# GpSimd's folding of the late rows' output, taken out of one stretch and put in two pieces behind the last PC of two segments

## The chip, the cores and the metric

One core of a Trainium2 chip runs the whole program. The metric is the device time of one execution in microseconds. The kernel before has a median of 838.83 us over 3 runs (838.33 to 838.89). TensorE is called PE, VectorE DVE, ScalarE ACT, GpSimd POOL, and the queue that issues nearly all DMAs is SyncE's, SP.

## What is computed

One sequence of 2048 tokens with 512 features passes through two layers. The first is attention with a recurrent memory: the sequence is cut into 64 segments of 32 tokens, and each segment sees 8 memory rows and itself. The memory rows of its output are the memory of the next segment, so the segments form a chain. The second layer is an MLP with 1792 hidden features.

```
for s in range(n_seg):
    xs = x[:, s * seg_len:(s + 1) * seg_len, :]
    h = jnp.concatenate([mem, xs], axis=1)
    q, k, v = (einsum('btd,dhe->bhte', h, W) for W in (Wq, Wk, Wv))
    p = softmax(where(mask, einsum('bhqe,bhke->bhqk', q, k) * scale, -1e9))
    o = einsum('bhte,hed->btd', einsum('bhqk,bhke->bhqe', p, v), Wo)
    mem = o[:, :M, :]
    outs.append(o[:, M:, :])
h = x + concatenate(outs)                 # on layernorm(x)
out = h + gelu(layernorm(h) @ w1 + b1) @ w2 + b2
```

## The kernel before

**Tiling.** Four segments make a block of 128 tokens; 16 blocks, 64 segments, numbered from 0. Of each segment, 24 token rows and the 8 memory rows go through Q, K and V in the segment itself (`hT`). The last 8 token rows of the four segments of a block, the late rows, are projected together, a block ahead (`hB`), in fill-in work that stands between the chained matmuls: the first segment of a block (called the first, sg = 0) carries K of the late rows of the next block, the second carries Q, the third V, and the fourth the output projection of the block before, `wo_B`.

**One segment on the chained path.** PE does Q and K (line 864; they wait for the memory rows `hT`, line 1169), the scores SC0 and SC1 (line 1029, which wait for POOL's copy `ZC`, line 919), V, then the two halves of the probabilities times V (called PV0 and PV1, lines 1067 and 1072, which wait for DVE's `PTC`), PVA (line 1135, the rows of the segment before, which waits for POOL's copies `BD`, line 1124), and the output projection (line 1163). DVE makes the softmax of each half in two `PC` (line 1054) and one transposition `PTC` (line 1056), and at the segment's end transposes the output out of PSUM (`TT`, line 1175) and adds its halves into `hT` for the next segment and into `opT` for the output (line 1169). ACT empties PSUM (`kq`, `VS`, `OT`, line 882) and computes the exponentials.

**The tail of a segment** (`sa_tail`) is done while the next one runs: POOL scales the probabilities of the 24 rows (`PA`, line 1118, behind DVE's `rsa`), DVE transposes them (`PTA`, line 1120), and POOL copies them to `BD` in four copies.

**The folding.** `wo_B` leaves the late rows' output of a block in PSUM as four partial sums on four groups of 32 partitions. DVE transposes it to `TTB` (line 1194; one buffer for all blocks), and POOL folds it, in two halves of the feature columns. Each half is a copy of 64 partitions to `TTS`, an add of 64 partitions, a copy of 32 partitions, and four narrow adds of 32 partitions into `opT` (lines 1198 to 1204). `nat` then transposes `opT` with a DMA (`oN`, line 1209), adds it to x on DVE (line 1212), takes mean and variance and writes the sum to memory (line 1219).

**What sets the order.** Every operation is recorded with what it reads and writes. A list scheduler (`Sched.schedule`) orders each engine's work by planned times (`PLAN`), or by rank for what has none, and puts an operation into the earliest gap that it models. PE's order is written by hand (`ORDERS`). `align` counts PE's instructions and pads with weight loads, so that each segment starts at a given place (`PHASE`) within stretches of 256 instructions; `pauses` lets PE wait for one of its own earlier matmuls behind such a boundary, and `windows` places DMAs between boundaries. `EARLY` lists loads and transpositions for the MLP that are done in the last segments.

**The end.** The last `wo_B` within the loop (block 14's late rows) is in segment 63. Behind the loop, PE does the first MLP matmuls (line 1323) and, between them, `wo` of segments 62 and 63, PVA of segment 63 and `wo_B` of block 15. Then follow the second MLP matmuls (line 1520) and three more rounds of both (lines 1513 and 1520).

Of the kernel before, what the change touches and what calls it, by code (L numbers as in the profile page):

```python
# [21 lines left out]
SORT = True  # L22
FETCH_N, FETCH_US = 256, 0.0
FETCH_AT, PADS, SLIP = 65, 8, 24
PHASE = (4, 68, 132, 196)
KEEP = True
WINDOWS, WIN_LO, WIN_HI = True, 1.0, -0.8
PAUSES, PAUSE_IN, PAUSE_US = 3, 64, 0.5
# [3 lines left out]


EARLY = {54: (("hx", 0, 0.1), ("hx", 1, 0.6)), 55: (("hn", 0, 0.1), ("hn", 1, 0.4), ("hx", 2, 0.8)), 56: (("hx", 3, 0.3), ("hn", 2, 0.7)),
         57: (("hn", 3, 0.1), ("w1", 0, 0.6)), 58: (("w1", 6, 0.2),), 59: (("w1", 1, 0.1), ("w1", 2, 0.8)), 60: (("w1", 3, 0.2), ("w1", 4, 0.5)), 61: (("w1", 5, 0.1),)}
ORDERS = ((('Q0', 0, 1), ('K0', 0, 1), ('Q0', 1, 2), ('K0', 1, 2), ('Q0', 2, 3), ('Q1', 0, 1), ('Q0', 3, 4), ('K0', 2, 4), ('Q1', 1, 4), ('K1', 0, 4), ('SC0', 0, 99), ('V0', 0, 1), ('V1', 0, 1), ('V0', 1, 4), ('F1', 0, 1), ('SC1', 0, 99), ('V1', 1, 2), ('F0', 0, 1), ('V1', 2, 3), ('F1', 1, 2), ('V1', 3, 4), ('PV0', 0, 99), ('PVA', 0, 99), ('F1', 2, 3), ('WO', 0, 2), ('PV1', 0, 99), ('WO', 2, 8), ('F1', 3, 4), ('SA', 0, 99), ('F0', 1, 4)),
# [585 lines left out]
def build_kernel(nc, A_x, A_mem0, A_Wq, A_Wk, A_Wv, A_Wo, B_w1, B_b1, B_w2, B_b2, out):  # L622
# [3 lines left out]
    with st:  # L626
# [499 lines left out]
        def pv_a(s):  # L1126
            par = s % 3

            def f(e):
                for k in range(8):  # L1130
                    for t in range(2):
                        rows = slice(64 * t, 64 * t + 64)
                        c0 = 192 * (k // 4) + 24 * (k % 4)
                        o = quad[:, 2 + t, c0:c0 + 120].rearrange("p (b q) -> p b q", q=24)[:, 0:5:4]
                        ins = e.matmul(o, VS[rows, par, k // 4, (k % 4) * E:(k % 4 + 1) * E], BD[rows, s % 2, k // 2, 2 * t:2 * t + 2, :, k % 2],
                                       start=(k == 0), stop=True, tile_position=(64 * t, 0), skip_group_check=True)
                return ins
            S.op("pe", f, reads=[("VS", par, 0), ("VS", par, 1)] + [("BD", s % 2, j) for j in range(4)], writes=AQ, dur=0.29, mode=MH, ni=32)
# [47 lines left out]
        def wo_B(bk, bank):  # L1186
            for q in range(8):
                def f(e, q=q):
                    for j in range(4):
                        ins = e.matmul(ps[bank][32 * j:32 * j + 32, :], OTB[:, bk % 2, slot(8 * j + q), :], WO[:, 8 * j + q, :], start=(q == 0), stop=(q == 7),  # L1190
                                       tile_position=(0, 32 * j), skip_group_check=True)
                    return ins
                S.op("pe", f, reads=[("WO", g, a) for g in range(8) for a in range(2)] + [("OTB", bk % 2, sg) for sg in range(4)], writes=[("ps", bank)], dur=0.2135, mode=MC, ni=8)
            S.op("dve", lambda e: e.transpose(TTB[:].rearrange("p c q t -> p (c q t)"), ps[bank][:, :]), reads=[("ps", bank)], writes=["TTB"], dur=t_dve(512) + 0.02)
            o = opT[:, bk % 2, :, :].rearrange("p c (s t) -> p c s t", s=4)[:, :, :, NA:SEG]
            for c in (0, 2):
                t = TTB[:, c:c + 2]
                S.narrow(S.op("pool", lambda e, t=t: e.tensor_copy(TTS[0:64], t[64:128]), reads=["TTB"], writes=["TTS"], dur=0.7))
                S.narrow(S.op("pool", lambda e, t=t: e.tensor_tensor(t[0:64], t[0:64], TTS[0:64], ALU.add), reads=["TTB", "TTS"], writes=["TTB"], dur=0.7))
                S.narrow(S.op("pool", lambda e, t=t: e.tensor_copy(TTS[0:32], t[32:64]), reads=["TTB"], writes=["TTS"], dur=0.7))  # L1200
                for q in range(4):
                    def f(e, c=c, q=q, t=t):
                        x, y = [v[0:32, :, q].rearrange("p c (s t) -> p c s t", s=4) for v in (t, TTS)]
                        return e.tensor_tensor(o[32 * q:32 * q + 32, c:c + 2], x, y, ALU.add)
                    S.narrow(S.op("pool", f, reads=["TTB", "TTS"], writes=[("opB", bk % 2)], dur=0.3))

        def nat(bk):

# [139 lines left out]
        for s in range(NS):  # L1348
# [194 lines left out]
        rest = {0: lambda: wo(NS, later[-1], mem=False), 2: lambda: nat(NTB - 2), 4: lambda: pv_a(NS - 1), 5: lambda: pv_a_ev(NS - 1), 7: lambda: wo_B(NTB - 1, later[-1]),  # L1543
                9: lambda: wo(NS + 1, later[0], mem=False), 11: lambda: nat(NTB - 1)}
        rest = dict(zip((0, 1, 3, 4, 6, 7, 9), rest.values()))
        for n, fc in enumerate(range(3, FC)):
# [84 lines left out]
```

## Time and profile before

| | |
|---|---|
| median of 3 runs | 838.83 us (838.33 to 838.89) |
| the profiled execution's own time | 839.32 us |
| its span | 837.6 us |
| PE busy | 786.5 us, 94% of the span |
| DVE busy | 638.3 us, 76% |
| ACT busy | 534.6 us, 64% |
| POOL busy | 347.9 us, 42% |
| a segment in the middle of the program | 10.4 to 11.4 us |

The profile is of one execution; its times are counted from the start of its span. A row of the timeline gives start and duration in us, engine, line and operation, tiles and shapes, how many instructions were merged into it, and in brackets how long the engine stood idle ahead of it and what ended that. PE's matmuls overlap, so a row's duration reaches into the next row; distances are best read from start to start. A row of waits gives the waiting instruction, what it waited for, the sum in us, how often, and the longest.

### The profile page before, as it was taken

Reading aid. Unit: us, or ns where it says so; the run is one execution under the profiler, and the core shown is the slowest. Engines: PE = TensorE matmul, PEld = TensorE weight load, DVE = VectorE, ACT = ScalarE, POOL = GpSimd, SP = SyncE. Lnnn points to the kernel's source line nnn. Section 1 sums busy time; section 2 is a strip of 40 time slices with the busy share of each in tenths; the row PEclk is TensorE's granted clock in tenths of the full one; section 3 lists DMA queues with packets and bytes.
Section 4 is the critical chain, followed back from the end, with each engine's and each line's share of the span. In section 5 each row is a group of like instructions: output and inputs, shape, how many; then the busy total and the mean of one; then the engine's idle time right before and its main releaser. Section 6 shows DMA issues by size and latency. Waiting matters only on the chain.

```text
span 837.6 us, 43562 instructions
## 1 busy us (share of the span) xinstructions
PE 786.5 (94%) x19317; PEld 424.5 (51%) x18882; DVE 638.3 (76%) x2022; ACT 534.6 (64%) x1496; POOL 347.9 (42%) x886
## 2 busy tenths in 40 slices
PE   3788999999999999999999999999999999889998
PEld 1355555555555555555555555555555554534443
DVE  3367888989898989888989898989898887713111
ACT  2536767777776767676767676767676768723332
POOL 5023235453535353535353535353535343446200
PEclk9999999999999999999999999999999999989999
DMA  9950010101010101011010101010112130363200
GB/s 342 389 159 9 4 36 10 41 17 36 21 36 16 37 21 35 23 24 33 20 38 20 38 17 41 13 39 10 42 35 67 33 93 16 114 162 96 62 26 25
DMA packets 65450, 48.03 MB, mean 57 GB/s; under 512 B 29029, under 2 KB 61677, under 8 KB 65261
## 3 DMA queue, kind: packets, MB, share of 16 engines
q1 hardware_dynamic: 64928, 44.98, 18.3%
q8 instruction: 150, 2.46, 1.3%
q10 hardware_dynamic: 332, 0.27, 0.1%
q14 instruction: 40, 0.32, 0.1%
HBM read 31.08 MB, written 8.13 MB: 47 GB/s over the span
## 4 chain that ended last, share of the span: by engine, by line
PE 64%; DVE 18%; ACT 8%; SPq 5%; issue 2%; POOL 1%; DMA 1%; POOLq 0%; DVEq 0%
PE ps L864 28%; PE ps L1163 12%; PE quad L1520 6%; DVE PC L1054 5%; PE ps L604 5%; PE ps L1513 4%; ACT EC L1046 4%; PE quad L1067 3%; SPq L791 2%; ACT kq L882 2%; SPq L774 2%; DVE nmc L1037 2%; DVE KALL L905 2%; PE quad L1029 2%; PE ps L1097 1%
## 5 line engine op out<-in xcount | busy, mean ns | idle before, releaser
L864 PE MATMUL ps<-WQ,hT 128*32 128x512 bf16 x2048 | 157.0, 380 | 6.6 <-DVE hT L1169 5.4
L1163 PE MATMUL ps<-WO,OT 128*32 128x256 bf16 x4224 | 141.8, 275 | 1.8 <-issue 1.0
L864 PE MATMUL ps<-WV,hT 128*32 128x512 bf16 x1780 | 142.6, 379 | 0.0
L1118 POOL TENSOR_TENSOR PA<-SA,rsa 128x256 bf16<-128x256 f32 x64 | 39.8, 622 | 220.7 <-DVE rsa L1111 209.1
L883 ACT ACTIVATE kq<-ps 128x512 bf16<-128x512 f32 x146 | 87.2, 597 | 62.9 <-PE ps L864 62.6
L882 ACT CAST kq<-ps 128x512 bf16<-128x512 f32 x160 | 93.4, 583 | 37.3 <-PE ps L864 37.3
L1163 PEld LDWEIGHTS ps<-WO,OT 128*32 128x32 bf16 x4224 | 96.3, 96 | 24.8 <-ACT OT L882 2.6
L1054 DVE SCALAR_TENSOR_TENSOR PC<-EC,rsc,even 128x128 bf16<-128x128 f32 x256 | 98.9, 411 | 4.4
L1124 POOL COPY BD<-PTA 32x192 bf16<-32x192 bf16 x256 | 92.4, 361 | 16.3 <-DVE PTA L1120 0.5
L864 PE MATMUL ps<-WK,hT 128*32 128x512 bf16 x1292 | 92.7, 379 | 0.0
L864 PEld LDWEIGHTS ps<-WQ,hT 128*32 128x32 bf16 x2048 | 58.3, 96 | 63.0 <-issue 18.1
L1046 ACT ACTIVATE EC<-quad,nmc 128x64 f32<-128x64 f32 x252 | 77.1, 311 | 10.1 <-DVE nmc L1037 3.6
L905 DVE STREAM_TRANSPOSE KALL<-kq 128x256 f32<-128x256 f32 x160 | 69.6, 435 | 16.2 <-ACT kq L882 13.4
L882 ACT CAST OT<-quad 128x128 bf16<-128x128 f32 (+1 forms) x207 | 67.2, 353 | 20.4 <-PE quad L1072 11.7
L604 PE MATMUL ps<-WK,hT 128*32 128x512 bf16 x756 | 75.0, 379 | 0.4 <-ACT kq L883 0.4
L882 ACT CAST VS<-ps 128x512 bf16<-128x512 f32 x126 | 73.8, 586 | 1.8
L864 PEld LDWEIGHTS ps<-WV,hT 128*32 128x32 bf16 x1780 | 51.5, 96 | 34.5 <-issue 2.0
L1109 ACT ACTIVATE SA<-SA 128x256 f32<-128x256 f32 x64 | 26.7, 417 | 55.4 <-DVE SA L1108 53.1
L1516 ACT ACTIVATE WQ<-ps,b1t 128x512 bf16<-128x512 f32 x42 | 28.9, 687 | 51.9 <-PE ps L1513 51.9
L905 DVE STREAM_TRANSPOSE QT<-kq 128x256 f32<-128x256 f32 x128 | 56.3, 440 | 6.1 <-ACT kq L883 4.3
L864 PEld LDWEIGHTS ps<-WK,hT 128*32 128x32 bf16 x1292 | 37.0, 97 | 46.0 <-issue 20.5
L1175 DVE STREAM_TRANSPOSE TT<-ps 128x256 f32<-128x256 f32 x66 | 28.9, 438 | 35.5 <-PE ps L1163 35.3
(161 smaller groups left out, 1501.6 us busy)
## 6 DMA issues: line engine op xcount, KB each, us to landing
WV<-in_A_Wv_dram SPq DMA_DIRECT2D x4, 1024.0 KB, 10.3
WK<-in_A_Wk_dram SPq DMA_DIRECT2D x4, 1024.0 KB, 18.3
WQ<-in_A_Wq_dram SPq DMA_DIRECT2D x4, 1024.0 KB, 19.0
WO<-in_A_Wo_dram SPq DMA_DIRECT2D x16, 256.0 KB, 7.5
v_last<-VSB SPq DMA_DIRECT2D x60, 64.0 KB, 3.1
VBD<-v_last SPq DMA_DIRECT2D x60, 64.0 KB, 2.8
h_mid<-xr SPq DMA_DIRECT2D x16, 128.0 KB, 1.9
WQ<-h_mid SPq DMA_DIRECT2D x4, 512.0 KB, 4.2
```

The source lines that it names most:

```text
L604: return e.add_instruction(mybir.InstMatmult(name="I-%d" % (4000000 + _kept[0]), engine=mybir.EngineType.PE, start_tensor_calc=start, stop ...
L864: ins = e.matmul(o, l, m, start=(k == 0), stop=(k == DC - 1), tile_position=(0, 32 * j), skip_group_check=True)
L882: return {"act": (lambda e: e.copy(out, src), t_act(n, ps_)), "dve": (lambda e: e.tensor_copy(out, src), 0.155 + 1.0e-3 * n * fast)}
L883: return {"act": (lambda e: e.mul(out, src, scale_), t_act(n, ps_)), "dve": (lambda e: e.tensor_scalar(out, src, scale_, None, ALU.mult), ...
L905: S.op("dve", lambda e: e.transpose(out, src), reads=[("kq", i)], writes=[key], dur=t_dve(256) + 0.02)
L1046: return e.activation(EC[:, r, sl, :], o[:, sl, :], ACTF.Exp, bias=nmc[:, r, sl:sl + 1], accum_out=smc[:, r, sl:sl + 1])
L1054: S.op("dve", lambda e, sl=sl, xc=xc: e.scalar_tensor_tensor(PC[:, r, :, :, sl], xc, rsc[:, r, sl:sl + 1], ev, ALU.mult, ALU.mult), reads= ...
L1118: S.either({k: ((lambda e: e.tensor_tensor(PA[:].rearrange("p a t b -> p a b t"), SA[:].rearrange("p (a b) t -> p a b t", b=2), bc2, ALU.m ...
L1124: S.narrow(S.op("pool", lambda e, j=j, rows=rows: e.tensor_copy(BD[rows, par, :, j, :, :], PTA[rows, :, 0:NA, :]), reads=["PTA"], writes=[ ...
L1163: ins = e.matmul(ps[bank][32 * j:32 * j + 32, 0:256], lhs(slot(h)), wo_cols(h, b), start=(k == 0), stop=(k == 15), tile_position=(0, 32 * ...
L1513: ins = e.matmul(ps[bank][:, 0:SBT], W1[:, cc, fc * P:(fc + 1) * P], hnT_of(k)[:, cc, :], start=(cc == 0), stop=(cc == DC - 1))
L1520: S.op("pe", lambda e: e.matmul(quad[:, t, :], gT_of(k, fc)[:, t * P:(t + 1) * P], W2[:, fc, :], start=(fc == 0), stop=(fc == FC - 1)), re ...
```

## The change

The folding becomes two functions, one for each half of the feature columns (`chunk(0, ...)` and `chunk(2, ...)`), which `wo_B` only puts on a list. They are recorded in the tails of the next two segments, the first and the second of the following block, and each may start only when the last `PCa` and `PC` of that segment are done. In the last segment, 63, both are recorded and also wait for the four copies `BD` of that segment. The folding of block 15 is recorded right behind its `wo_B`, as before. `nat` of a block moves from the first to the third segment, behind the folding. `PHASE` is 4 instructions less everywhere, and one transposition and one load of `EARLY` come later.

```diff
-PHASE = (4, 68, 132, 196)
+PHASE = (0, 64, 128, 192)
...
-         57: (("hn", 3, 0.1), ("w1", 0, 0.6)), 58: (("w1", 6, 0.2),), 59: ...
+         57: (("w1", 0, 0.6),), 58: (("hn", 3, 0.2), ("w1", 6, 0.4)), 59: ...
...
-            for c in (0, 2):
+
+            def chunk(c, after):
                 t = TTB[:, c:c + 2]
-                S.narrow(S.op("pool", lambda e, t=t: e.tensor_copy(TTS[0:64], t[64:128]), reads=["TTB"], writes=["TTS"], dur=0.7))
+                S.narrow(S.op("pool", lambda e: e.tensor_copy(TTS[0:64], t[64:128]), reads=["TTB"], writes=["TTS"], dur=0.4, after=after))
...
+            folds.extend([lambda after: chunk(0, after), lambda after: chunk(2, after)])
+
+        folds = []
+
+        def fold(after=()):
+            tag, S.tag = S.tag, None
+            folds.pop(0)(after)
+            S.tag = tag
...
-            if sg == 0 and bk > 1:
+            if sg == 2 and bk > 1:
                 nat(bk - 2)
...
                 sa_tail(s)
+                if folds and s % 4 < 2 or s == NS - 1:
+                    for _ in folds[:1 if s < NS - 1 else 2]:
+                        fold([S.last_writer[(n, 1)] for n in ("PC", "PCa")] + [S.last_writer[("BD", s % 2, j)] for j in range(4 * (s == NS - 1))])
...
-        rest = {..., 7: lambda: wo_B(NTB - 1, later[-1]),
+        rest = {..., 7: lambda: (wo_B(NTB - 1, later[-1]), fold(), fold()),
```

How the instructions stand on POOL around the folding of one block, in the kernel before. The first row is the end of the first half, which follows the copies `BD` of the fourth segment; each `PA` opens the tail of one more segment, here that of the first, done while the second runs:

```order
L1204 TENSOR_TENSOR opT<-TTB,TTS 32x8x8 x4
L1198 COPY TTS<-TTB 64x256
L1199 TENSOR_TENSOR TTB<-TTB,TTS 64x256
L1200 COPY TTS<-TTB 32x256
L1204 TENSOR_TENSOR opT<-TTB,TTS 32x8x8
L1118 TENSOR_TENSOR PA<-SA,rsa 128x4x2x32
L1204 TENSOR_TENSOR opT<-TTB,TTS 32x8x8
L919 COPY ZC<-QT 128x8x2x8
L926 COPY ZC<-QTB 128x16x2x8
L919 COPY ZC<-QT 128x8x2x8
L1124 COPY BD<-PTA 32x4x48 x4
L1204 TENSOR_TENSOR opT<-TTB,TTS 32x8x8 x2
```

The same place with the change:

```order
L1124 COPY BD<-PTA 32x4x48 x4
L1199 COPY TTS<-TTB 64x256
L1200 TENSOR_TENSOR TTB<-TTB,TTS 64x256
L1201 COPY TTS<-TTB 32x256
L1205 TENSOR_TENSOR opT<-TTB,TTS 32x8x8 x4
L1118 TENSOR_TENSOR PA<-SA,rsa 128x4x2x32
L919 COPY ZC<-QT 128x8x2x8
L926 COPY ZC<-QTB 128x16x2x8
L919 COPY ZC<-QT 128x8x2x8
L1124 COPY BD<-PTA 32x4x48 x4
L1199 COPY TTS<-TTB 64x256
```

Before, both halves followed one another behind the copies `BD` of one segment's tail, and the last narrow adds stood between the next segment's `PA` and `ZC` and behind its `BD`. Now one half follows each of two segments' copies, none stands between `PA` and `ZC`, and its first copy waits for DVE as well.

POOL at the end of segment 63, before; the second row is the start of the folding of block 14:

```order
L1124 COPY BD<-PTA 32x4x48 x4
L1198 COPY TTS<-TTB 64x256
L1199 TENSOR_TENSOR TTB<-TTB,TTS 64x256
L1200 COPY TTS<-TTB 32x256
L1204 TENSOR_TENSOR opT<-TTB,TTS 32x8x8 x4
L1118 TENSOR_TENSOR PA<-SA,rsa 128x4x2x32
```

and with the change:

```order
L1124 COPY BD<-PTA 32x4x48 x4
L1118 TENSOR_TENSOR PA<-SA,rsa 128x4x2x32
L1124 COPY BD<-PTA 32x4x48 x4
L1199 COPY TTS<-TTB 64x256
L1200 TENSOR_TENSOR TTB<-TTB,TTS 64x256
L1201 COPY TTS<-TTB 32x256
L1205 TENSOR_TENSOR opT<-TTB,TTS 32x8x8 x4
```

`PA` and the copies `BD` of segment 63 have moved ahead of the two halves of the folding.

DVE at the same place, before and with the change (`WV` here is the normalised x of the MLP's second round, `TTB` in the last row that of block 15):

```order
L1111 RECIPROCAL rsa<-sma 128x8
L1169 TENSOR_TENSOR opT<-TT 64x4x24 x2
L1267 TENSOR_SCALAR WV<-WQ,agg,rst 128x512 x3
L1175 STREAM_TRANSPOSE TT<-ps 128x256
L1169 TENSOR_TENSOR opT<-TT 64x4x24 x2
L1267 TENSOR_SCALAR WV<-WQ,agg,rst 128x512
L1120 STREAM_TRANSPOSE PTA<-PA 128x128
```

```order
L1111 RECIPROCAL rsa<-sma 128x8
L1169 TENSOR_TENSOR opT<-TT 64x4x24 x2
L1276 TENSOR_SCALAR WV<-WQ,agg,rst 128x512
L1120 STREAM_TRANSPOSE PTA<-PA 128x128
L1276 TENSOR_SCALAR WV<-WQ,agg,rst 128x512
L1175 STREAM_TRANSPOSE TT<-ps 128x256
L1169 TENSOR_TENSOR opT<-TT 64x4x24 x2
L1276 TENSOR_SCALAR WV<-WQ,agg,rst 128x512 x2
L882 CAST OT<-quad 128x16x24
L1194 STREAM_TRANSPOSE TTB<-ps 128x512
```

`PTA` stands behind one normalisation instead of four and behind two adds instead of four. PE's matmuls stand in the same order in both kernels, but for four weight loads of padding less in segment 1.

More of the change, by code (lines that the diff above doesn't have):

```diff
@@ L1195, in wo_B, with f @@
             o = opT[:, bk % 2, :, :].rearrange("p c (s t) -> p c s t", s=4)[:, :, :, NA:SEG]
-            for c in (0, 2):
+            def chunk(c, after):
                 t = TTB[:, c:c + 2]
-                S.narrow(S.op("pool", lambda e, t=t: e.tensor_copy(TTS[0:64], t[64:128]), reads=["TTB"], writes=["TTS"], dur=0.7))
-                S.narrow(S.op("pool", lambda e, t=t: e.tensor_tensor(t[0:64], t[0:64], TTS[0:64], ALU.add), reads=["TTB", "TTS"], writes=["TTB"], dur=0.7))
-                S.narrow(S.op("pool", lambda e, t=t: e.tensor_copy(TTS[0:32], t[32:64]), reads=["TTB"], writes=["TTS"], dur=0.7))
+                S.narrow(S.op("pool", lambda e: e.tensor_copy(TTS[0:64], t[64:128]), reads=["TTB"], writes=["TTS"], dur=0.4, after=after))
+                S.narrow(S.op("pool", lambda e: e.tensor_tensor(t[0:64], t[0:64], TTS[0:64], ALU.add), reads=["TTB", "TTS"], writes=["TTB"], dur=0.73))
+                S.narrow(S.op("pool", lambda e: e.tensor_copy(TTS[0:32], t[32:64]), reads=["TTB"], writes=["TTS"], dur=0.41))
                 for q in range(4):
-                    def f(e, c=c, q=q, t=t):
+                    def f(e, q=q):
                         x, y = [v[0:32, :, q].rearrange("p c (s t) -> p c s t", s=4) for v in (t, TTS)]
                         return e.tensor_tensor(o[32 * q:32 * q + 32, c:c + 2], x, y, ALU.add)
-                    S.narrow(S.op("pool", f, reads=["TTB", "TTS"], writes=[("opB", bk % 2)], dur=0.3))
+                    S.narrow(S.op("pool", f, reads=["TTB", "TTS"], writes=[("opB", bk % 2)], dur=0.31))
+            folds.extend([lambda after: chunk(0, after), lambda after: chunk(2, after)])
[4 more added lines that the diff above has]
+            S.tag = tag
         def nat(bk):
@@ L1542, in build_kernel @@
         early, later = (free + sorted(set(busy)))[:2], (free + sorted(set(busy)))[2:]
-        rest = {0: lambda: wo(NS, later[-1], mem=False), 2: lambda: nat(NTB - 2), 4: lambda: pv_a(NS - 1), 5: lambda: pv_a_ev(NS - 1), 7: lambda: wo_B(NTB - 1, later[-1]),
+        rest = {0: lambda: wo(NS, later[-1], mem=False), 2: lambda: nat(NTB - 2), 4: lambda: pv_a(NS - 1), 5: lambda: pv_a_ev(NS - 1), 7: lambda: (wo_B(NTB - 1, later[-1]), fold(), fold()),
                 9: lambda: wo(NS + 1, later[0], mem=False), 11: lambda: nat(NTB - 1)}
```

2 lines of the change are left out of this document (1 added, 1 removed).

## The prediction

> **What bounds the kernel now.** I read the chain of waits first, then who waited for whom on PE, then the timeline of single segments against each other, then the end of the loop.
>
> ```profile
> PE 64%; DVE 18%; ACT 8%; SPq 5%; issue 2%; POOL 1%; DMA 1%; POOLq 0%; DVEq 0%
> PE quad L1067 <- DVE PTC L1056: 6.5, 25, 0.7
> PE quad L1135 <- POOL BD L1124: 4.7, 1, 4.7
> PE ps L1163 <- issue: 1.0, 2, 0.7
> PE ps L864 <- issue: 0.7, 3, 0.3
> ```
>
> PE carries most of the chain; the other engines count where they release it. One wait stands out: PE waited once for 4.7 us, at PVA, for POOL's copies `BD`. And 25 times it waited for `PTC` ahead of PV0 or PV1, 6.5 us in all.
>
> How long a segment is, from the first Q matmul of one to that of the next:
>
> ```profile
> 82.72 0.41 PE L864 MATMUL ps<-WQ,hT 128*32 128x512 bf16 x4 [0.77 <-DVE hT L1169]
> 93.55 0.40 PE L864 MATMUL ps<-WQ,hT 128*32 128x512 bf16 x4
> 103.86 0.41 PE L864 MATMUL ps<-WQ,hT 128*32 128x512 bf16 x4
> ...
> 403.38 0.41 PE L864 MATMUL ps<-WQ,hT 128*32 128x512 bf16 x4
> 413.75 0.41 PE L864 MATMUL ps<-WQ,hT 128*32 128x512 bf16 x4
> 424.11 0.41 PE L864 MATMUL ps<-WQ,hT 128*32 128x512 bf16 x4
> 435.48 0.40 PE L864 MATMUL ps<-WQ,hT 128*32 128x512 bf16 x4
> 446.00 0.41 PE L864 MATMUL ps<-WQ,hT 128*32 128x512 bf16 x4
> ```
>
> The row at 424.11 opens the first segment of a block: it lasts 11.37 us, the second (435.48) 10.52, the third (403.38) 10.37. The first three rows are the first and second segment of block 1, which have no folding yet: 10.83 and 10.31. So a first segment is 0.54 longer and a second 0.21 longer than without a folding and without the transposition into `TTB`, which stays. That is the ceiling of what the loop can give: 0.75 for each folding.
>
> ```profile
> L1204 POOL TENSOR_TENSOR opT<-TTB,TTS x128: 306/313/398, 132.5 to 750.8; 32x64 bf16<-32x64 f32 x128
> ```
>
> 128 narrow adds, 8 a folding, are 16 foldings: 14 lie in a first and second segment (blocks 2 to 15), one at the end of segment 63, one behind the loop.
>
> **The end of the loop.** In the last segment the folding is not beside the path but on it:
>
> ```profile
> 726.87 0.20 DVE L1111 RECIPROCAL rsa<-sma 128x8 f32<-128x8 f32 x1
> 727.10 0.96 DVE L1169 TENSOR_TENSOR opT<-TT 64x96 bf16<-64x96 f32 x2
> 728.07 1.25 DVE L1267 TENSOR_SCALAR WV<-WQ,agg,rst 128x512 bf16<-128x512 bf16 x3
> 734.04 0.31 DVE L1120 STREAM_TRANSPOSE PTA<-PA 128x128 f32<-128x128 f32 x1 [2.68 <-POOL PA L1118]
> ...
> 726.66 0.39 POOL L1198 COPY TTS<-TTB 64x256 f32<-64x256 f32 x1 [5.81 <-DVE TTB L1194]
> 733.38 0.62 POOL L1118 TENSOR_TENSOR PA<-SA,rsa 128x256 bf16<-128x256 f32 x1 [0.17 <-POOL opT L1204]
> 734.48 1.54 POOL L1124 COPY BD<-PTA 32x192 bf16<-32x192 bf16 x4 [0.48 <-DVE PTA L1120]
> ...
> 730.35 1.02 PE L1323 MATMUL ps<-xr,QTB 128*128 128x512 bf16 x4
> 736.08 0.50 PE L1135 MATMUL quad<-BD,VS 64*128 64x48 bf16 x16 [4.71 <-POOL BD L1124]
> 736.52 1.89 PE L1323 MATMUL ps<-xr,QTB 128*128 128x512 bf16 x4
> ...
> 82.00:92.00 10.00, 9.26 (x244) 5.56 (x299) 8.16 (x29) 6.61 (x20) 3.12 (x8) 1.00 0.01 3
> 736.00:741.70 5.70, 5.62 (x28) 2.02 (x28) 1.86 (x4) 1.85 (x3) 0.82 (x3) 0.50 0.77 130
> ```
>
> `rsa` is ready at 727.07, but POOL began the folding at 726.66 and takes `PA` only at 733.38. `PTA`, the copies `BD` and at 736.08 PVA follow, while PE had run dry 4.71 us earlier, at 731.37. The last two rows are from a table by stretches (the column behind POOL's is the granted clock): from 736.00 to 741.70 PE has a clock of 0.50, against 1.00 in an early stretch, and the same four matmuls take 1.89 us instead of 1.02. So the wait costs 4.71 and half of 5.7 behind it, 2.8: 7.5 us.
>
> With the change `PA` and `BD` come ahead of the folding. `PA` runs from 727.1 to 727.75. On DVE, `PTA` then stands behind two adds (0.96 at most, the row of before, which lay beside the folding) and one normalisation (1.25 for three, so 0.42): 727.07 + 1.38 + 0.31 = 728.8. The copies take 1.54: `BD` is ready at 730.3, and PE asks for it at 731.37. Cover 1.07 us; what exceeds it would be lost one for one. I take the whole **7.5 us**; the low end, if the wait only moves to another place, is in the rivals.
>
> What becomes late instead: the folding of block 14 (6.55 us, from 726.66 to `PA`'s 733.38 less 0.17) now runs from 730.3 to 736.9, 3.7 us later by the clock, with PE 7.5 earlier. On it hang `TTB` of block 15 (one buffer), and SP, which waits for it in order:
>
> ```profile
> 733.24 1.20 SPq L1209 DMA_TRANSPOSE oN<-opT  x1
> 734.49 5.19 SPq L1278 DMA_TRANSPOSE WQ<-WV  x4
> 745.66 3.38 SPq L1535 DMA_DIRECT2D WK<-in_B_w_dram  x4
> ...
> 761.26 4.66 PE L1513 MATMUL ps<-WQ,WK 128*128 128x512 bf16 x20
> ```
>
> The transposition of block 14's output moves from 733.24 to 737.0; behind it are the four transpositions for the MLP's second round (to 743.4) and, with a second such wait for the folding of block 15 (`TTB` from 737, then 6.55 of folding, to about 744.3), the last `w1` loads, issued by 749. PE wants the second round at 761.26 - 7.5 = 753.8: 4.8 us of cover for the first matmul, more for the late columns. Cost nothing; without that cover each us is lost.
>
> **The first segment.** The folding lies beside the softmax of the second half:
>
> ```profile
> 430.81 0.72 POOL L1199 TENSOR_TENSOR TTB<-TTB,TTS 64x256 f32<-64x256 f32 x1
> ...
> 409.90 0.63 DVE L1054 SCALAR_TENSOR_TENSOR PC<-EC,rsc,even 128x128 bf16<-128x128 f32 x2
> 430.97 1.18 DVE L1054 SCALAR_TENSOR_TENSOR PC<-EC,rsc,even 128x128 bf16<-128x128 f32 x2
> 434.84 0.49 DVE L1169 TENSOR_TENSOR hT<-TT 64x32 bf16<-64x32 f32 x2
> 444.17 0.53 DVE L1169 TENSOR_TENSOR opT<-TT 64x96 bf16<-64x96 f32 x2
> 445.06 0.45 DVE L1175 STREAM_TRANSPOSE TT<-ps 128x256 f32<-128x256 f32 x1 [0.37 <-PE ps L1163]
> 445.55 0.39 DVE L1169 TENSOR_TENSOR hT<-TT 64x32 bf16<-64x32 f32 x2
> ...
> 432.55 0.27 PE L1067 MATMUL quad<-PTC,VS 64*128 64x32 bf16 x8 [0.32 <-DVE PTC L1056]
> 431.93 1.26 ACT L882 CAST OT<-quad 128x384 bf16<-128x384 f32 x3
> 438.26 0.32 POOL L1204 TENSOR_TENSOR opT<-TTB,TTS 32x64 bf16<-32x64 f32 x1
> ```
>
> The two `PC` take 1.18 us beside POOL's adds and copies, 0.63 in the third segment. With the folding behind them 0.55 goes from DVE, of which PE can use the 0.32 that it stood idle ahead of PV1. Not all of that comes through: the third of ACT's three casts reads PV1's result, and ACT is busy with the other two, which don't, until about two thirds of 1.26, 432.8; the second half of the output projection waits for that cast. Of 0.32 I take **0.2** (bounds 0 and the 0.54 above). The memory adds at the end, 0.49 here against 0.39 at 445.55, keep their 0.10: half a folding is 3.3 us and now runs from about 431.6 to 434.9, so it still reaches them.
>
> **The second segment.** A narrow add of 0.32 no longer stands between `PA` and `ZC` (438.26), and none behind `BD`: at most the 0.21 above. But half a folding now runs from about 442.8 to 446.0, beside the adds at 444.17 and 445.55. Beside the folding two such adds took 0.96 (727.10), 0.43 more than here; the 0.37 that DVE idles ahead of `TT` hides that but for 0.06, and the memory adds get the 0.10 of the first segment. That leaves 0.21 - 0.16 = **0.05**; the low end, if the memory adds slow like those at 727.10 (0.39 x 0.96/0.53, 0.32 more), is -0.17.
>
> The rest of the edits I take as nothing. `nat`'s transposition moves to the third segment, its reader on DVE stands in the fourth, so a whole segment covers it. Of `EARLY`, one transposition moves by a segment, its reader is PE in segment 60; uncovered it would cost one such DMA issue (1.20) and its landing, once. `PHASE` moves the boundaries by four instructions: PE's waits on issue are 1.7 us in all, so at best that is gained, and I put the same on the other side.
>
> **Sum.** 14 x (0.2 + 0.05) = 3.5, and 7.5 at the end: 11.0 us. The profiled execution took 839.3 (837.6 of span and 1.7 around it), which gives 828.3; the median of the runs is 0.5 below the profiled one, so **827.8 us**.
>
> **The rivals.**
> 1. The loop gives nothing. POOL's half foldings slow the ends of two segments as much as they free the middle of one. For it: ACT's casts stand close behind DVE's chain, and the memory adds are the last link into the next segment. Against: block 1's segments are shorter. 838.8 - 7.5 = 831.3 us.
> 2. The loop gives its ceiling, 14 x 0.75 = 10.5: 838.8 - 7.5 - 10.5 = 820.8. Against: `TTB`'s transposition remains, and the half foldings still run.
> 3. The end only moves its wait: PE runs into the MLP's second round while SP still stands behind the two foldings. Price at most what SP's order allows: if the 749 above became 757, 3.2 us past 753.8: 831.0. For it: SP serves in order, and two of its entries now wait for POOL. For a wait that is shortened but not gone, the rows say that 0.77 of idling (at 82.72) leaves the clock at 1.00 (the stretch from 82 to 92) and 4.71 doesn't. The Trainium skill, "TensorE: Matmul & The Clock Gate", Part 1, puts the limit at about 3.4 us of idling; by it a wait of 3.2 would add no slow clock, and 831.0 would stand; the 4.71 agrees with it, and no row here shows a wait between.
> 4. Slower: in each of the 28 segments both memory adds are held until a narrow add of POOL (0.31) has ended, 0.62 instead of the 0.10 counted, about 0.5 more on the last link: 827.8 + 28 x 0.5 = 841.8. It decides from 0.4 a segment (11.0/28), and it stands in the row at 430.97, where a `PC` paid nearly double. Against: at 434.84 the adds met a copy and lost 0.10. The Trainium skill, "SBUF — State Buffer", section "SBUF: two separate sides", has this rule: a DVE operation with two SBUF inputs and a GpSimd operation that reads SBUF exclude each other for a whole instruction. By it this rival would be the forecast; the rows agree for `PC` and only in part for the memory adds.
>
> **Chances.** The forecast 0.63, with a range of its own of 824.5 to 830.5 (the boundaries' 1.7 and 1 to 1.5 of the loop on either side); rival 1 0.18, rival 2 0.07, rival 3 0.08, rival 4 0.04. The range of 8 in 10 is 823.5 to 831.8: above it takes in rivals 1 and 3, below a loop that gives 0.56 a folding (7.8) instead of 0.25 (3.5). What can be told from no change here is 0.2%, 1.7 us. Faster is everything but rival 4 and 0.02 of rival 3, for an end that gives all back: 0.94; the same 0.02; slower 0.04.
>
> **What would show it.** PVA of segment 63 without a wait and PE's clock at 1.00 through the end of the loop; `PA` there right behind `rsa`, about 6 us ahead of the folding's end. First segments of about 11.17 us, with the two `PC` at 0.63 and no wait ahead of PV1 larger than before; second segments of about 10.47, without POOL's add between `PA` and `ZC`, and with the two memory adds at about 0.5. The third and fourth as before. Wrong would be: memory adds of 0.6 or more, first segments of 11.3 or more, or a new wait of PE at line 1513.

## The result and the profile after

The changed kernel has a median of 829.28 us (828.36 to 829.8) beside 838.86 us of the kernel before; the ratio is 0.9886, interval 0.9869 to 0.9903. The same kernel in a later job: 828.32 us (827.85 to 829.45) beside 839.74, 0.9866 (0.9853 to 0.988). So it is some 10 us faster; forecast were 11.0 us and 827.8. The profiled execution took 829.1 us with a span of 827.4, 10.2 less than before.

**The waits of PE after the change** (engine, line, what it waited for, sum in us, times, longest):

```profile
PE ps L864 <- DVE hT L1169: 5.7, 8, 1.1
PE quad L1067 <- DVE PTC L1056: 2.3, 12, 0.2
PE quad L1029 <- POOL ZC L919: 2.1, 12, 0.2
```

Two rows are to be compared with before: the wait for `BD` (4.7) is gone from the list, and the 25 waits for `PTC` of 6.5 us have become 12 of 2.3.

**The end of the loop**, POOL, DVE and PE in the timeline (start, duration, engine, line):

```profile
724.02 0.20 DVE L1111 RECIPROCAL rsa<-sma 128x8 f32<-128x8 f32 x1
724.40 0.62 POOL L1118 TENSOR_TENSOR PA<-SA,rsa 128x256 bf16<-128x256 f32 x1 [6.40 <-DVE rsa L1111]
725.47 0.30 DVE L1120 STREAM_TRANSPOSE PTA<-PA 128x128 f32<-128x128 f32 x1
725.91 1.57 POOL L1124 COPY BD<-PTA 32x192 bf16<-32x192 bf16 x4 [0.89 <-DVE PTA L1120]
727.54 0.39 POOL L1199 COPY TTS<-TTB 64x256 f32<-64x256 f32 x1
...
732.53 1.49 POOL L1205 TENSOR_TENSOR opT<-TTB,TTS 32x64 bf16<-32x64 f32 x4
...
727.43 1.02 PE L1332 MATMUL ps<-xr,QTB 128*128 128x512 bf16 x4
728.38 0.37 PE L1135 MATMUL quad<-BD,VS 64*128 64x48 bf16 x16
728.69 1.04 PE L1332 MATMUL ps<-xr,QTB 128*128 128x512 bf16 x4
...
751.04 0.59 PE L1525 MATMUL ps<-WQ,WK 128*128 128x512 bf16 x2
```

And the same stretches as in before's table (length, busy time of PE, PEld, DVE, ACT and POOL with instructions, then the granted clock, DMA share, GB/s):

```profile
726.00:732.00 6.00, 6.00 (x51) 2.31 (x53) 2.58 (x7) 4.10 (x7) 5.15 (x13) 1.00 0.78 243
732.00:738.00 6.00, 6.00 (x104) 3.14 (x96) 2.32 (x5) 1.73 (x3) 4.28 (x12) 1.00 0.30 69
```

`PA` now stands right behind `rsa`, `BD` is ready at 727.48, and the folding runs from 727.54 to 734.02. PVA (728.38) has no wait in brackets, and PE is busy through both stretches at clock 1.00. From the first matmul with `QTB` to the first of the second round (line 1513, now 1525) it was 761.26 - 730.35 = 30.91 us and is 751.04 - 727.43 = 23.61: 7.30 us less, and no wait has come up at the second round.

**A first and a second segment** in the middle of the program, the openings on PE and then what DVE and POOL do within them:

```profile
422.52 0.41 PE L864 MATMUL ps<-WQ,hT 128*32 128x512 bf16 x4
433.74 0.40 PE L864 MATMUL ps<-WQ,hT 128*32 128x512 bf16 x4
444.16 0.41 PE L864 MATMUL ps<-WQ,hT 128*32 128x512 bf16 x4
454.53 0.41 PE L864 MATMUL ps<-WQ,hT 128*32 128x512 bf16 x4
...
429.38 0.63 DVE L1054 SCALAR_TENSOR_TENSOR PC<-EC,rsc,even 128x128 bf16<-128x128 f32 x2
433.04 0.55 DVE L1169 TENSOR_TENSOR hT<-TT 64x32 bf16<-64x32 f32 x2
443.68 0.41 DVE L1169 TENSOR_TENSOR hT<-TT 64x32 bf16<-64x32 f32 x2
...
430.13 0.39 POOL L1199 COPY TTS<-TTB 64x256 f32<-64x256 f32 x1 [1.46 <-DVE PC L1054]
430.61 0.72 POOL L1200 TENSOR_TENSOR TTB<-TTB,TTS 64x256 f32<-64x256 f32 x1
431.86 1.49 POOL L1205 TENSOR_TENSOR opT<-TTB,TTS 32x64 bf16<-32x64 f32 x4
```

The first segment lasts 11.22 (11.37 before), the second 10.42 (10.52), the third 10.37 as before. The two `PC` at 429.38 take 0.63 for 1.18 before, and POOL's folding begins just behind them. Its narrow adds (from 431.86 to 433.35) reach into the memory adds at 433.04, which take 0.55. All `PC` together, a row by line (busy time, mean ns of one):

```profile
L1054 DVE SCALAR_TENSOR_TENSOR PC<-EC,rsc,even 128x128 bf16<-128x128 f32 x256 | 90.5, 378 | 4.4
```

Summed over segments 8 to 59, the 13 first segments give 1.9 us, the 13 second ones 1.3 (0.55 of it from a single one that lasted 10.98 in before); the third ones cost 0.4. The fourth ones are 1.0 shorter, but this differs between executions: in part it hangs on whether the copies from `xT` on POOL meet a `PC`.

### The profile page after: what moved, and what is told of

It is laid out like the page before. It is cut to its first block, busy times and chain, and to the rows that moved or that the text cites. A ratio compares the mean times of both kernels' runs of the same rounds, so it can differ in the third digit from the quotient of the medians.

```text
span 827.4 us, 43568 instructions
## 1 busy us (share of the span) xinstructions
PE 786.6 (95%) x19317; PEld 425.3 (51%) x18878; DVE 637.3 (77%) x2022; ACT 530.9 (64%) x1496; POOL 349.0 (42%) x886
## 4 chain that ended last, share of the span: by engine, by line
PE 64%; DVE 19%; ACT 8%; SPq 5%; issue 2%; DMA 1%; POOL 1%; DVEq 0%; POOLq 0%
PE ps L864 27%; PE ps L1163 13%; PE quad L1532 6%; PE ps L604 4%; PE ps L1525 4%; ACT EC L1046 4%; DVE PC L1054 4%; ACT kq L882 3%; PE quad L1067 3%; SPq L791 2%; DVE KALL L905 2%; SPq L774 2%; DVE nmc L1037 2%; PE ps L1332 1%; PE ps L1097 1%
## 5 line engine op out<-in xcount | busy, mean ns | idle before, releaser
L864 PE MATMUL ps<-WQ,hT 128*32 128x512 bf16 x2048 | 160.1, 383 | 6.5 <-DVE hT L1169 5.7
L1124 POOL COPY BD<-PTA 32x192 bf16<-32x192 bf16 x256 | 94.4, 369 | 16.7 <-DVE PTA L1120 0.9
L864 PE MATMUL ps<-WK,hT 128*32 128x512 bf16 x1292 | 94.5, 381 | 0.0
L1054 DVE SCALAR_TENSOR_TENSOR PC<-EC,rsc,even 128x128 bf16<-128x128 f32 x256 | 90.5, 378 | 4.4
L1046 ACT ACTIVATE EC<-quad,nmc 128x64 f32<-128x64 f32 x252 | 76.8, 310 | 10.2 <-DVE nmc L1037 3.7
L604 PE MATMUL ps<-WK,hT 128*32 128x512 bf16 x756 | 76.7, 380 | 0.4 <-ACT kq L883 0.4
L1584 DVE TENSOR_TENSOR WV<-quad,WV 128x512 bf16<-128x512 f32 x16 | 11.1, 692 | 51.8 <-PE quad L1532 48.1
```

The costliest lines, as they stand in the source:

```text
L604: return e.add_instruction(mybir.InstMatmult(name="I-%d" % (4000000 + _kept[0]), engine=mybir.EngineType.PE, start_tensor_calc=start, stop ...
L864: ins = e.matmul(o, l, m, start=(k == 0), stop=(k == DC - 1), tile_position=(0, 32 * j), skip_group_check=True)
L1046: return e.activation(EC[:, r, sl, :], o[:, sl, :], ACTF.Exp, bias=nmc[:, r, sl:sl + 1], accum_out=smc[:, r, sl:sl + 1])
L1054: S.op("dve", lambda e, sl=sl, xc=xc: e.scalar_tensor_tensor(PC[:, r, :, :, sl], xc, rsc[:, r, sl:sl + 1], ev, ALU.mult, ALU.mult), reads= ...
L1124: S.narrow(S.op("pool", lambda e, j=j, rows=rows: e.tensor_copy(BD[rows, par, :, j, :, :], PTA[rows, :, 0:NA, :]), reads=["PTA"], writes=[ ...
```

## The experiments

Each has a ratio to the kernel before as it ran in the same job.

**1. The changed kernel again** (no edit).

> The changed kernel once more. Theory: the two stretches in which the profile of after granted half the clock in the opening (37.79 to 44.61 and 51.44 to 54.85 us) against one in before (42.01 to 45.42) come and go from run to run, and are no part of the change: the rounds scatter by about 1 us around 829.3 us, and a second profile shows another pattern, segments 0 and 1 shorter by up to 1.1 us. Rival: the change causes them (4 pad loads fewer in segment 1): the same stretches again, segments 0 and 1 again 1.1 us longer than in before.

Measured: 828.32 us. The opening of the program, the stretches where the clock fell, in the first profile and in the second (the last three columns: granted clock, DMA share, GB/s). First profile of after:

```profile
34.00:46.00 12.00, 8.37 (x196) 4.37 (x190) 5.37 (x19) 5.52 (x19) 0.74 (x2) 0.72 1.09 353
50.00:55.00 5.00, 4.21 (x48) 2.58 (x100) 2.91 (x10) 1.18 (x2) 2.69 (x8) 0.66 0.37 89
```

Second profile:

```profile
34.00:46.00 12.00, 7.42 (x188) 4.41 (x192) 5.33 (x20) 5.49 (x19) 0.74 (x2) 0.86 1.09 352
50.00:55.00 5.00, 4.39 (x100) 2.97 (x148) 3.90 (x13) 2.34 (x5) 3.44 (x11) 1.00 0.35 87
```

0.66 in one execution and 1.00 in the other, of the same kernel, in the same five microseconds. The first profile was 1.1 us longer in segments 0 and 1 than before's, the second 0.3 shorter. In the profiles of the kernels below these two segments lie between 0.6 us less and 1.2 us more than in before. It is no part of the change, and it may be a part of the scatter of 1 to 1.5 us between executions.

**2. The end alone, as I thought.** The kernel before with segment 63 as in the change. In code: the changed kernel, with

```diff
-            if sg == 2 and bk > 1:
+            if sg == 0 and bk > 1:
                 nat(bk - 2)
...
                     wo_B(bk - 1, BANK["FB"])
+                    for _ in range(2 * (s < NS - 1)):
+                        fold()
```

and `PHASE` and `EARLY` as before. The operations of the folding kept the durations that the change records them with.

> The kernel before with the change in segment 63 alone (folding behind BD); loop, PHASE, EARLY and nat as before. Theory (end and loop are two separate gains): before less 7.3 to 7.5 us, 831.4 us; PVA of segment 63 without a wait for BD and the clock at 1.00 through the end of the loop; segments 8 to 59 as in before (first ones 11.37, second ones 10.52). Rival 1 (the end's gain needs PHASE or EARLY too): a wait of over 1 us is left ahead of PVA or ahead of line 1520, 833 us or more. Rival 2 (the end is worth the whole): 829.3 us.

Measured: 827.5 us (826.67 to 828.38), 0.9855 (0.984 to 0.987): all that the change gives and a little more, with no piece in the loop waiting for a `PC`. The theory failed, and rival 2 had the time but not the cause: the end gave its 7.3 us, and the loop got shorter too. The openings of a first, a second and a third segment, and POOL and DVE in the first:

```profile
422.40 0.41 PE L864 MATMUL ps<-WQ,hT 128*32 128x512 bf16 x4
433.57 0.40 PE L864 MATMUL ps<-WQ,hT 128*32 128x512 bf16 x4
443.95 0.41 PE L864 MATMUL ps<-WQ,hT 128*32 128x512 bf16 x4
...
424.00 0.40 POOL L1199 COPY TTS<-TTB 64x256 f32<-64x256 f32 x1 [1.86 <-DVE TTB L1194]
424.58 0.62 POOL L1118 TENSOR_TENSOR PA<-SA,rsa 128x256 bf16<-128x256 f32 x1 [0.18 <-DVE rsa L1111]
428.67 0.72 POOL L1200 TENSOR_TENSOR TTB<-TTB,TTS 64x256 f32<-64x256 f32 x1
433.25 1.53 POOL L1205 TENSOR_TENSOR opT<-TTB,TTS 32x64 bf16<-32x64 f32 x4
429.29 0.77 DVE L1054 SCALAR_TENSOR_TENSOR PC<-EC,rsc,even 128x128 bf16<-128x128 f32 x2
```

11.17 and 10.38 us. The folding's first copy has moved ahead of `PA`, into POOL's idle time, and the rest ends 1.2 us behind the opening of the second segment, so nothing of it lies between `PA` and `ZC` or behind the next `BD`. The 64-partition add at 428.67 overlaps the second half's `PC` (429.29) by 0.1 us only, and the two take 0.77, for 1.18 before: the folding is not off this softmax, but its large add nearly is. This kernel differs from the one I meant in one thing that I had overlooked: the planner was told 0.4 for a copy instead of 0.7, and the copy fits a gap in which it didn't fit before. Experiments 5 and 6 take the two things apart.

**3. The loop alone.** The changed kernel with the folding of segment 63 recorded at once, ahead of `PA`:

```diff
                     wo_B(bk - 1, BANK["FB"])
+                    for _ in range(2 * (s == NS - 1)):
+                        fold()
```

> The changed kernel, but block 14's folding in segment 63 is recorded ahead of PA and BD as in before; the loop, PHASE, EARLY and nat as in the change. Theory: before less 14 x (0.16 + 0.10) = 3.6 us and whatever boundaries and opening add (0 to 1.3), 835.3 to 836.5 us; first segments 11.21, second ones 10.42, PVA of segment 63 waits 4 to 5 us for BD again. Rival (the loop gives nothing): 838.9 us.

Measured: 835.2 us, 0.9949 (0.9937 to 0.9962), 4.3 us of 839.74 (3.2 to 5.3). The wait of PVA for `BD` is back with 4.8 us. The loop's part is worth about what was forecast, and the rival is out.

**4. The wait for the last PC taken out.** The order on POOL is that of the change; only in the loop the first copy no longer waits for `PC`:

```diff
-fold([S.last_writer[(n, 1)] for n in ("PC", "PCa")] + [S.last_writer[("BD", s % 2, j)] ...
+fold([S.last_writer[(n, 1)] for n in ("PC", "PCa")[:2 * (s == NS - 1)]] +
+     [S.last_writer[("BD", (s if s == NS - 1 else s - 1) % 2, j)] for j in range(4)])
```

> The changed kernel, but the two pieces in the loop wait only for what is ahead of them on POOL (the copies BD of the segment before), no longer for the segment's last PC; POOL's order is the same to the instruction, segment 63 as in the change. Theory (the place behind the PC is what pays, because POOL's folding and DVE's PC slow each other): in first segments the PC of the second half at 0.5 to 0.7 us again, PV1 at 8.4 and the length 11.37 as in before; in second segments the same two PC are hit too, PV1 0.3 to 0.5 late, length 10.7 to 10.9: after plus 14 x (0.16 + 0.3 to 0.5), 835.7 to 838.5 us. Rival (the cut into two is what pays, the wait for the PC does nothing): 829.3 us, lengths as in the change, since the folding that begins 1.3 us earlier is then also off the memory adds and the first segments are 11.08.

Measured: 838.92 us, 0.9987 (0.9978 to 0.9996), beside 828.32 of the change in the same job: in the cut kernel the wait alone is worth 10.6 us, as much as the whole change. The openings of a first, a second and a third segment, then DVE and POOL in another second segment, then the row of all `PC`:

```profile
471.82 0.41 PE L864 MATMUL ps<-WQ,hT 128*32 128x512 bf16 x4
483.09 0.40 PE L864 MATMUL ps<-WQ,hT 128*32 128x512 bf16 x4
494.13 0.41 PE L864 MATMUL ps<-WQ,hT 128*32 128x512 bf16 x4
...
446.30 1.38 DVE L1054 SCALAR_TENSOR_TENSOR PC<-EC,rsc,even 128x128 bf16<-128x128 f32 x2
...
446.34 0.73 POOL L1200 TENSOR_TENSOR TTB<-TTB,TTS 64x256 f32<-64x256 f32 x1
447.13 0.39 POOL L1201 COPY TTS<-TTB 32x256 f32<-32x256 f32 x1
...
L1054 DVE SCALAR_TENSOR_TENSOR PC<-EC,rsc,even 128x128 bf16<-128x128 f32 x256 | 108.8, 449 | 4.4
```

First segments 11.27, second ones 11.04. Two `PC` beside the folding take 1.38 instead of 0.63, while POOL's add keeps its 0.73. The first segment loses only 0.05 to 0.2 against the change, because the folding that starts earlier is off the memory adds; the second loses 0.62, more than the 0.3 to 0.5 expected. A cut without a wait is worse than no cut: this kernel has the gain of the end (PVA of segment 63 does not wait), and yet it is only some 1 us faster than before. Beside experiment 6, which has the same end and the loop of before, it is some 5.7 us slower (0.9987 and 0.9919): both halves then meet a softmax, and in second segments the two `PC` at issue, 1.38 here, took 0.63 in before.

**5. The four durations alone.** The kernel before with

```diff
-... writes=["TTS"], dur=0.7))
-... writes=["TTB"], dur=0.7))
-... writes=["TTS"], dur=0.7))
+... writes=["TTS"], dur=0.4))
+... writes=["TTB"], dur=0.73))
+... writes=["TTS"], dur=0.41))
...
-... writes=[("opB", bk % 2)], dur=0.3))
+... writes=[("opB", bk % 2)], dur=0.31))
```

> The kernel before with nothing but the four durations that the folding is recorded with, as in the change (0.4, 0.73, 0.41, 0.31 for 0.7, 0.7, 0.7, 0.3). It moves the folding's first copy ahead of PA, into POOL's idle time at the start of first segments, and one more narrow add and the rest of the folding 0.5 us earlier; segment 63 keeps its order (folding ahead of PA and BD). Theory (in end_alone the durations, which it kept from the change, moved the loop's folding and gave 4.5 of its 11.7 us): first segments 11.16, second ones 10.39, 14 x (0.18 + 0.13) = 4.3 us less than before, 835.0 us beside 839.3 (834.5 to 836); PVA of segment 63 still waits 4 to 5 us. Rival (the loop's gain in end_alone came from the edit in its last segment or by chance): 838 to 840 us, first segments 11.37.

Measured: 833.46 us, 0.9933 (0.992 to 0.9945), 5.6 us of 838.95 (4.6 to 6.7). First segments 11.14, second ones 10.38 or 10.51; PVA of segment 63 still waits 4.8 us. In the profile the first and second segments of blocks 2 to 14 give 4.1 us, beside 3.2 and 2.8 in the two profiles of the change. Another 0.9 lies at the end, where the same wait was followed by less time at the slow clock (29.99 us from the first `QTB` matmul to the second round, for 30.91); no run shows that the durations cause this. So four numbers in the planner's model, with no other edit, give about what the loop's part of the change gives.

**6. The end alone, with the old durations** (experiment 2 with 0.7, 0.7, 0.7 and 0.3; up to segment 62 every engine's order is that of before).

> The kernel before with the folding of segment 63 behind BD and the old durations: up to segment 62 every engine's order is that of before. Theory: before less 7.3 to 7.5 us, 831.5 to 832.3 us; segments 8 to 59 as in before. Rival (the end is worth what end_alone showed): 827.5 us.

Measured: 832.26 us, 0.9919 (0.9906 to 0.9933), 6.8 us less than 838.95 (5.6 to 7.9); the profiled span is 7.3 less than before's. First segments 11.36, second ones 10.51. PVA in the timeline:

```profile
730.41 1.02 PE L1332 MATMUL ps<-xr,QTB 128*128 128x512 bf16 x4
731.37 0.37 PE L1135 MATMUL quad<-BD,VS 64*128 64x48 bf16 x16
```

PVA stands at 731.37, the very time at which PE ran dry before. End and loop are two separate gains, and together (6.8 + 4.3) they make up the change (9.6 and 11.4 in its two jobs).

**7. The last narrow add of each piece behind the memory adds.**

```diff
+                    if q == 3:
+                        after = after + late
...
-... dur=0.31))
+... dur=0.31, after=after if q == 3 else ()))
...
+ fold(..., [S.last_writer[("hTm", (s + 1) % RING)]] * (s < NS - 1))
```

> The changed kernel with the last narrow add of each piece behind the memory adds of its segment (lines 1205 and 1169). Theory (in first segments that narrow add, at 10.51 after the segment's start beside the memory adds at 10.52, makes the first memory add 0.35 instead of 0.19): first memory add 0.19, first segments 11.08 where they were 11.21, 0.13 x about 9 of 13 to 14 = 1.2 us less than after's 828.3 to 829.3, 827.1 to 828 us. Rival (the memory adds are held by something else, or PE's next start does not hang on them): 11.21 again, 828.3 us or more.

Measured: 827.4 us (827.08 to 827.53), 0.9861 (0.9848 to 0.9875). DVE and POOL at the end of a first segment:

```profile
431.90 0.39 DVE L1169 TENSOR_TENSOR hT<-TT 64x32 bf16<-64x32 f32 x2
430.72 1.09 POOL L1207 TENSOR_TENSOR opT<-TTB,TTS 32x64 bf16<-32x64 f32 x3
432.43 0.32 POOL L1207 TENSOR_TENSOR opT<-TTB,TTS 32x64 bf16<-32x64 f32 x1 [0.63 <-DVE hT L1169]
```

The memory adds are back at 0.39, and all 13 first segments of blocks 2 to 14 last 11.03 to 11.06, where they scattered between 11.07 and 11.23. In time that is 0.9 us less than 828.32, within the expectation, but the intervals of the two ratios overlap; the lengths show it, the medians alone would not.

**8. A faster kernel, first attempt.** Experiment 2 with the output adds of the fourth segment's rows moved from the start of the first segment to behind its last `PTC`:

```diff
+                if s % 4 == 3 and s < NS - 1:
+                    held.append(rows)
+                else:
+                    rows()
...
                 sa_tail(s)
+                if s % 4 == 0 and held:
+                    held.pop()([S.last_writer[("PTC", 1)]])
```

> end_alone, with the output adds of every fourth segment's 24 rows (opT, line 1169), which stand at 2.04 to 2.91 in first segments ahead of the first QT, put behind that segment's last PTC. It is an attempt at a faster kernel. Theory (these adds, of which the second takes 0.61 beside PA on POOL, hold QT and with it SC0, 3.84 beside 3.45 in second segments): SC0 at 3.5, first segments 10.8 to 10.9, 14 x 0.27 to 0.37 = 3.8 to 5.2 us less than end_alone's 827.5: 822.3 to 823.7 us. Rival 1 (QT then waits for kq on ACT, or SC0 for POOL's ZC): 11.1, 827 us. Rival 2 (the adds at 8.0 to 9.0 meet POOL's folding and push the prefills and TT): first segments longer than 11.2, 828 us or more.

Measured: 827.88 us, 0.9869 (0.9853 to 0.9884): nothing gained on 827.5. SC0 came at 3.47 as forecast, but PV1 only 0.27 earlier (7.84), since the earlier softmax now met POOL's 64-partition add, and the output projection ended at 10.0 as ever: the adds at 7.8 to 8.5 had pushed a cast `OT` behind them on DVE. It is rival 2's mechanism, at the price of the gain and no more.

**9. Second attempt.** Experiment 7 with the same adds behind the segment's last cast `OT`:

```diff
+                    held.pop()([S.last_writer[("OTm", s % 2, 1)]])
```

> late_last, with the output adds of the fourth segment's rows (opT, line 1169) put in first segments behind the segment's last cast OT, not behind PTC as in opA_late. Theory (SC0 comes 0.37 earlier, as opA_late showed, no PC meets the folding, and the casts and prefills on ACT and DVE keep their places): SC0 at 3.46, PV1 at 7.6 to 7.75, first segments 10.65 to 10.75 beside 11.05: 14 x 0.3 to 0.4 = 4.2 to 5.6 us less than late_last's 827.4, 821.8 to 823.2 us, faster than every kernel so far. Rival (first segments end by ACT's casts, at 10.0 whatever PV1 does): line 1097 at 10.0 again, 827 us.

Measured: 823.04 us (822.36 to 823.5), 0.9803 (0.9789 to 0.9818), some 5 us less than the change, faster than both kernels. The openings, and DVE at the start of the first segment and behind its casts:

```profile
420.35 0.41 PE L864 MATMUL ps<-WQ,hT 128*32 128x512 bf16 x4
431.07 0.40 PE L864 MATMUL ps<-WQ,hT 128*32 128x512 bf16 x4
...
422.15 0.20 DVE L1111 RECIPROCAL rsa<-sma 128x8 f32<-128x8 f32 x1
422.73 0.45 DVE L905 STREAM_TRANSPOSE QT<-kq 128x256 f32<-128x256 f32 x1 [0.37 <-ACT kq L883]
428.76 0.63 DVE L1169 TENSOR_TENSOR opT<-TT 64x96 bf16<-64x96 f32 x2 [0.26 <-ACT OT L882]
429.89 0.45 DVE L1177 STREAM_TRANSPOSE TT<-ps 128x256 f32<-128x256 f32 x1 [0.50 <-PE ps L1163]
```

First segments last 10.55 to 10.89, with a median of 10.67. The first `QT` now waits for ACT, not for DVE, and the adds at 428.76 lie in DVE's idle time ahead of `TT`.

**10. PHASE as before in the changed kernel** (one line, (4, 68, 132, 196)).

> The changed kernel with PHASE as before, 4 instructions more everywhere. Theory (PHASE weighs nothing: the late first WQ and the meetings of the xT copies with PC at block boundaries come and go from run to run): 828.3 to 829.3 us, 0 within 0.9 us. Rival (PHASE sets where the code blocks are fetched, and part of the change's gain is from it): 830 us or more, with segments of one kind all longer by the same amount; or faster than 827.4.

Measured: 828.17 us (827.54 to 830.6), 0.9872 (0.9853 to 0.9891). No difference from the change that can be told.

**11. Both pieces in the first segment.**

```diff
-                if folds and s % 4 < 2 or s == NS - 1:
-                    for _ in folds[:1 if s < NS - 1 else 2]:
+                if folds and s % 4 < 1 or s == NS - 1:
+                    for _ in folds[:2]:
```

> The changed kernel with both pieces one behind the other in the first segment, the first behind that segment's last PC as in the change; segment 63 as in the change. POOL then has the second half's narrow adds around PA and, as in the kernel before, two of them behind the copies BD of the second segment, beside its PC. Theory (what pays is that no piece lies beside a PC; the cut itself only keeps the second half off PA and the next PC): first segments 11.2 as in the change, second ones 10.6 to 10.75 (PA 0.4 us late, two PC of 0.36 at 0.5): after plus 14 x 0.2 to 0.3, 831 to 833.5 us. Rival 1 (one piece would have done): 828.3 to 829.3 us. Rival 2 (PA and the narrow adds hold ZC and BD in second segments by over 0.5 us): 836 us or more.

Measured: 829.56 us (828.11 to 830.87), 0.9883 (0.9865 to 0.99): rival 1, it cannot be told from two pieces. First segments 11.08; second ones 10.51, 0.1 longer than in the change, a third to a half of what I expected, since of the first half's `PC` only one is lengthened (0.43 for 0.36). That is 1.3 us over the program, of which about half is given back at two places named below (segments 53 and 58). The first segments give back about 1 us more: 12 of 13 last 11.07 to 11.09 here, while in each profile of the change 8 of 13 last 11.2 or more.

## Why the prediction was right, point by point

**The end, 7.5 us.** Right in place and mechanism: `PA` right behind `rsa`, PVA without a wait, the clock at 1.00. 7.3 us in the traces, 6.8 (5.6 to 7.9) with the end changed alone. My estimate put `BD` at 730.3, 1.07 us ahead of PE's asking; it was ready at 727.48, 0.9 ahead of PVA at 728.38, both earlier by what the loop had saved. Rival 3 did not occur: PE came to the second round 23.61 us behind the first `QTB` matmul without a wait. The 2.8 for the slow clock was read from one execution: dur_only, with a wait of 4.77, lost 0.9 less. That the clock falls after 4.71 us of idling and not without it agrees with the Trainium skill, "TensorE: Matmul & The Clock Gate", Part 1, which puts the limit at about 3.4 us. A wait between 0.77 and 4.71 was not seen at this place, so the limit was not tried.

**The loop, 14 x (0.2 + 0.05) = 3.5 us.** The sum holds: 3.2 in the profile of after, 4.3 (3.2 to 5.3) in loop_alone. Its parts were sized a little off, and that they add up so well is in part luck: 0.55 of the 3.2 is the one long second segment of before. Against the 11.37 of most in before, first segments gained 0.15 to 0.29 for 0.2: PV1 came 0.36 earlier, the end of the output projection 0.21, as the step on ACT's casts said. The spread is from the memory adds: 0.35 and 0.19 where the last narrow add had started 0.01 to 0.02 us ahead of them, 0.19 and 0.22 where it had not. late_last, which moves that one add, takes it away. Second segments gained 0.10 for 0.05: the memory adds there took 0.41, not 0.49. The ceiling of 0.54 stood on weak ground: it rests on one segment of 10.83 without a folding, the first of block 1, and the same segment lasted 11.09 and 10.55 in the two profiles of the change.

**What I gave as its cause was only half of it.** The step "with the folding behind them 0.55 goes from DVE" is right, and behind_BD shows it from the other side: without the wait for `PC` the loop is 10.6 us longer than with it. But the change carries another edit, the four durations told to the planner, which my account of the change left out. They are part of the diff and looked like bookkeeping. In dur_only they alone move the folding's first copy into idle time and give 5.6 us. So there are two ways. The wait puts the folding behind the second softmax (two `PC` at 0.63). The right durations leave it there, but move its large add ahead of it (0.77, for 1.18 before) and its end out of the way of the second segment's `ZC` and `BD`. In the changed kernel the place is set by the wait. That the folding is cut in two was not needed: one_stretch does as well.

**Rival 4** asked for memory adds of 0.62 each time; they took 0.56 at most and 0.39 to 0.41 in many segments. The rule of the Trainium skill, "SBUF — State Buffer", section "SBUF: two separate sides", that a DVE operation with two SBUF inputs and a GpSimd operation that reads SBUF hold each other off for a whole instruction, agrees in part: two `PC` lost 0.75 beside an add of 0.73 and the copies next to it (1.38 for 0.63), but a memory add lost 0.16 beside a narrow add of 0.31 that had begun 0.01 ahead of it, not 0.31. POOL's own add lost nothing.

**EARLY, nat and PHASE at nothing.** PHASE was right (phase_back). `nat` in the third segment was costed at nothing because a whole segment covers its transposition; the cost was elsewhere, in its add on DVE. In segment 58 of after it comes 5.7 us behind the segment's opening, between the last `PC` of the first half and `PTC`; in before and in one_stretch it comes at 2.0:

```profile
662.09 0.36 DVE L1054 SCALAR_TENSOR_TENSOR PC<-EC,rsc,even 128x128 bf16<-128x128 f32 x1
662.35 0.57 DVE L1221 TENSOR_TENSOR xr<-xr,oN 128x512 bf16<-128x512 bf16 x1
662.84 0.30 DVE L1056 STREAM_TRANSPOSE PTC<-PC 128x128 f32<-128x128 f32 x1
663.28 0.27 PE L1067 MATMUL quad<-PTC,VS 64*128 64x32 bf16 x8 [0.39 <-DVE rsc L1051]
```

PE idles 0.39, and the segment lasts 10.83 for 10.48. Segment 53, a second one, lost 0.3 to 0.4 in the same kernels: the output adds there take 0.88 beside the folding, and one more normalisation stands behind them, so the 0.37 us of DVE's idling that I took as cover was used up. Together 0.7 us, once each. In one_stretch and end_alone, where no folding runs in second segments at that time, both segments have their old lengths (10.51 or 10.38, and 10.48): so it is the second piece that costs this, and it is a part of why one stretch can't be told from two.

**Against 829.28.** The change's two profiles save 7.3 at the end and 2.8 to 3.2 in first and second segments, less the 0.4 of segment 58: 9.7 to 10.1 of the 11.0 forecast. Two more differences stand in the profiles, and nothing shows that they come from the change: the opening was 1.1 us longer in the first one and 0.3 shorter in the second, and the fourth segments were 1.0 and 0.7 shorter. How they share in the two medians, 829.28 and 828.32, no run shows.

## What to carry to other kernels

Where two engines slow each other, ask for each long off-path operation which short on-path operation it lies beside, and start it behind that one; here the wait alone was worth as much as the whole change, and a cut without it was worse than none. Check the durations that a planner is given against the profile before rewriting an order: here the kernel with four of them set right was 5.6 us faster. And read every number in a diff as an edit that can move instructions, also where it looks like tidying.

## What the hardware showed that I had not expected

Two operations that overlap by nearly the same amount do not cost the same: the memory add took 0.19 or 0.35 depending on whether the narrow add on POOL began just after or just before it, and so first segments of one kernel last 11.08 or 11.21. Cut free of that neighbour (late_last) all of them agree within 0.03.

The loss is one-sided for the large operations: POOL's 64-partition add took 0.72 to 0.73 beside `PC` or alone, while the `PC` pair went from 0.63 to 1.38, although the first of them had begun 0.04 ahead of the add (446.30 and 446.34 in behind_BD). With the copies `BD` it went both ways: in first segments the `PC` beside one paid (0.51 for 0.36), in second ones the copy did (0.50 for 0.34). In the first case both begin at 428.33, in the second the `PC` begins 0.05 ahead of the copy (439.20 and 439.25). That the one which begins first is spared would fit these and the narrow adds, but not the `PC` at 446.30; what decides it was not tried.
